# Routing totals from small matmuls, the key sums' column sums a step later, and one subtraction of the maxima per step

## The chip, the cores and the metric

The kernel runs on one core of a Trainium2 chip. The metric is the device time of one execution in microseconds. Five engines work side by side: TensorE (PE, with its weight loads listed apart as PEld), VectorE (DVE), ScalarE (ACT), GpSimd (POOL) and SyncE (SP), which issues most of the transfers. SBUF is the on-chip memory, PSUM the memory that TensorE writes its results to.

## The reference

Three layers follow one another. The first is linear attention with a softmax-like feature map, the second sends each token to one of eight experts, the third is a dense layer with a norm. Cut to what matters here:

```python
def phi(x):                                  # q, k: (8, 8, 576, 64), w_phi: (64, 128)
    proj = np.einsum('bhsd,df->bhsf', x, w_phi)
    proj = proj - np.max(np.abs(proj), axis=-1, keepdims=True)
    return np.concatenate([np.exp(proj), np.exp(-proj)], axis=-1)
q_p, k_p = phi(q), phi(k)
kv = np.einsum('bhsf,bhsd->bhfd', k_p, v)
z = np.sum(k_p, axis=2)                      # sum over the keys
num = np.einsum('bhsf,bhfd->bhsd', q_p, kv)
den = np.einsum('bhsf,bhf->bhs', q_p, z)[..., None] + 1e-06
x = num / den                                # 4608 tokens of 512

logits = x @ w_gate + modality_bias[modality_id]
e_idx = np.argmax(logits, axis=1)            # one expert of 8 for each token
gate_w = softmax(logits)[arange(N), e_idx]
for e in range(E):                           # w1[e]: 512 x 1024, w2[e]: 1024 x 512
    out[mask] = gate_w[mask, None] * (np.maximum(x[mask] @ w1[e], 0.0) @ w2[e])
# then h = out @ w_in, h * softmax(h), a norm, @ w_out
```

## The kernel before, in words

The attention part fills the first 347 us or so. Its work comes in 8 units (a pair of batch entries `p2` and one of two groups of four heads `g`); a unit has two halves (the two batch entries) and 9 jobs, and each job is one step of the main loop, so there are 72 steps. A step does the following. `project` multiplies a piece of keys and a piece of queries by `w_phi` (16 matmuls, L186) into the PSUM tile `pj`. DVE takes the largest absolute value of each group of 128 features (L191) and `features` subtracts it from `pj`, once for the keys (`xsk`) and once for the queries (`xsq`), both L196. ACT takes the two exponentials of the keys (`e`, L203 and L204). Two steps later (`LAGF`) `q_features` transposes the queries (L256) and ACT takes their exponentials (`qp`, L263), and `accum_kv` adds keys times values to the PSUM tile `kv` (L209). POOL adds the key features to a running sum `es` (L248; L224 for the 64 leftover rows of two batch entries), which starts as zeros (L217).

When a half is complete, `finish_kv` copies `kv` to `kt` on ACT (L251) and puts items on a list: two `kf_part` (kind "f", L330, copied to `kf` by ACT, L334), one `z_part` and four or five `tokens`, all of kind "64". `z_part` is 32 matmuls of one column each with `es` as weights (L310, "tp<-used,es" in the rows, called the z columns here); `es` must be complete for them. `tokens` multiplies 128 tokens' `qp` by `kf` (64 matmuls in two halves of PE, L310, "tp<-kf,qp"), and DVE divides by the denominator and writes the token rows `xt` and the gate logits `gs` (L409 to L415). At most two items of kind "64" (`COLS`) and two "f" (`FULL`) run in a step. `z_part` is ready one step after its half is complete.

After the second unit of a pair, `gating` runs for 4 or 5 token tiles (9 times in all; 36 tiles): DVE finds the expert of each token as a one-hot table `oh` (L427 to L441), two matmuls (L449 with a triangle of ones, L450 with all ones) count the tokens of the same expert ahead of each token in its tile, and in the whole tile; both go to one PSUM tile `rkp`, which ACT copies to `rk` (L455). DVE then runs a chain over the tiles: `base` starts as the running totals `cnt` (L468), each tile's totals are added to the one before (L470, one operation for a tile), and the sum of `rk` and `base` (L475) gives each token's place, with which POOL scatters the rows to the table `xe` in HBM (L482, `g_dsti` holds the places).

After the gating of the fifth batch pair's second half, `early.pick` (L694 to L706, tiles `ea_`) chooses the expert whose weights are loaded first; its result `ea_tab` is read by SP, which then issues the loads of these weights into `ldk`, `ldq` and `ldv` (L733, in `prefetch`, step `PRE` of the last unit). At step `STEP0` of the last unit the first weight tile is split into a rounded part on ACT (L776) and the rest on DVE (L777). `setup_bias` computes the routing bias on POOL at step `BIAS` (L103 to L113). The last tiles run in `finish_last`, with the first expert's matmuls (`first_slot`, L515, and its maximum with zero on DVE, L519) between them. From about 360 us on PE runs the expert and dense matmuls (L932), which the change does not touch.

PE's order is the order of the code in the attention part. DVE, ACT, POOL and SP get their order there from the compiler's scheduler, so an edit moves instructions on them that it does not name. PSUM tiles of the names `tp` come from a pool of 3 (`tps`), `pj` of 2, `kv` of 1.

## Time and profile before

| what | value |
|---|---|
| time, median of 3 runs | 1204.37 us (1201.35 to 1208.66) |
| profiled execution, own time | 1209.89 us |
| its span in the trace | 1207.7 us |
| mean granted clock of TensorE | 0.985 |
| PE busy | 1166.4 us (97%) |
| DVE busy | 842.5 us (70%) |
| ACT busy | 576.9 us (48%) |
| POOL busy | 404.1 us (33%) |

PE is busy nearly all the time, but the 41 us in which it is idle lie almost wholly in the first 360 us, so the views to read are those of that part: the timeline of PE with the idle time ahead of each operation and what ended it, and the windows, where PEclk tells at what share of full speed the clock was granted (about 0.5 is 1.2 GHz, 1.00 is 2.4 GHz). The profiled execution was 5.5 us slower than the median run.

### The profile page before, as it was taken

Reading aid. Unit: us, or ns where it says so; the run is one execution under the profiler, and the core shown is the slowest. Engines: PE = TensorE matmul, PEld = TensorE weight load, DVE = VectorE, ACT = ScalarE, POOL = GpSimd, SP = SyncE. Lnnn points to the kernel's source line nnn. Section 1 sums busy time; section 2 is a strip of 40 time slices with the busy share of each in tenths; the row PEclk is TensorE's granted clock in tenths of the full one; section 3 lists DMA queues with packets and bytes.
Section 4 is the critical chain, followed back from the end, with each engine's and each line's share of the span. In section 5 each row is a group of like instructions: output and inputs, shape, how many; then the busy total and the mean of one; then the engine's idle time right before and its main releaser. Section 6 shows DMA issues by size and latency. Waiting matters only on the chain.

```text
span 1207.7 us, 27753 instructions
## 1 busy us (share of the span) xinstructions
PE 1166.4 (97%) x10658; PEld 1017.8 (84%) x10658; DVE 842.5 (70%) x1606; ACT 576.9 (48%) x974; POOL 404.1 (33%) x460
## 2 busy tenths in 40 slices
PE   7998999997989999999999999999999999999997
PEld 5787887886879999999999999977777778888885
DVE  6689889798666577787777877665655565566561
ACT  6455554655443455555555654643434343444342
POOL 4967867866640000000000000123233333433331
PEclk9899999999899999999999999999999999999999
DMA  9523433332231322145231324787877856556541
GB/s 322 181 80 123 137 95 120 123 122 80 86 111 62 83 86 71 53 133 166 57 85 54 88 67 129 200 206 206 226 202 202 224 136 149 147 134 151 148 119 48
DMA packets 249657, 157.40 MB, mean 130 GB/s; under 512 B 168752, under 2 KB 227376, under 8 KB 249520
## 3 DMA queue, kind: packets, MB, share of 16 engines
q1 hardware_dynamic: 243472, 136.39, 41.4%
q0 software_dynamic: 5760, 19.03, 4.1%
q8 instruction: 86, 1.41, 0.5%
q14 instruction: 51, 0.42, 0.1%
q10 hardware_dynamic: 288, 0.16, 0.0%
HBM read 167.12 MB, written 51.37 MB: 181 GB/s over the span
## 4 chain that ended last, share of the span: by engine, by line
PE 41%; DMA 6%; issue 1%; ACT 1%; DVE 1%; SPq 1%; POOLq 0%; ACTq 0%; DVEq 0%
PE tp L932 20%; PE h L932 19%; DMA turned<-whi 2%; DMA wlo<-turned 2%; DMA gd<-xe 1%; PE tp L1251 1%; SPq L1102 1%; DMA ldk<-in_moe_w_dram 1%; PE tp L747 0%; DMA gt<-gd 0%; DMA yd<-yo 0%; PE tp L1235 0%; DMA out_dram<-wab,gt 0%; ACT ex L1121 0%; ACT whi L1153 0%
## 5 line engine op out<-in xcount | busy, mean ns | idle before, releaser
L777 POOL TENSOR_TENSOR yTl<-yin,yTh 128x512 fp32r<-128x512 f32 x36 | 47.4, 1317 | 415.4 <-PE tp L932 403.1
L248 POOL TENSOR_TENSOR es<-es,e 128x512 f32<-128x512 f32 x128 | 162.1, 1273 | 50.6 <-ACT e L204 43.4
L932 PE MATMUL tp<-xTh,whi 128*128 128x256 f32 x432 | 122.1, 283 | 2.3 <-PEq L1332 2.3
L932 PE MATMUL h<-hTh,wlo 128*128 128x256 f32 x432 | 120.4, 279 | 0.8 <-DVE wlo L777 0.8
L932 PE MATMUL h<-hTl,whi 128*128 128x256 f32 x432 | 120.5, 279 | 0.4 <-DVE hTl L947 0.4
L932 PE MATMUL tp<-xTl,whi 128*128 128x256 f32 x432 | 120.9, 280 | 0.0
L932 PE MATMUL tp<-xTh,wlo 128*128 128x256 f32 x432 | 120.9, 280 | 0.0
L932 PE MATMUL h<-hTh,whi 128*128 128x256 f32 x432 | 120.3, 279 | 0.0
L191 DVE TENSOR_REDUCE m<-pj 128x8 f32<-128x1024 f32 x72 | 87.7, 1219 | 40.7 <-PE pj L186 39.8
L263 ACT ACTIVATE qp<-tp 128x512 f32<-128x512 f32 x128 | 69.1, 593 | 71.8 <-PE tp L256 68.9
L1121 ACT ACTIVATE ex<-h,s_mx,gt 128x1024 f32<-128x1024 f32 x36 | 43.5, 1208 | 124.1 <-DVE s_mx L1118 66.8
L1116 DVE TENSOR_REDUCE s_mx<-h 128x1 f32<-128x512 f32 x72 | 46.4, 686 | 78.6 <-PE h L932 78.6
L1134 POOL TENSOR_SCALAR rs<-s_var,gt 128x1 f32<-128x1 f32 x36 | 12.4, 344 | 227.1 <-ACT sq L1131 227.1
L1131 ACT ACTIVATE sq<-ex 128x1024 bf16<-128x1024 f32 x36 | 38.1, 1058 | 97.9 <-DVE ex L1128 97.9
L932 PEld LDWEIGHTS tp<-xTh,whi 128*128 128x128 f32 x432 | 81.9, 189 | 2.5 <-issue 2.4
L932 PEld LDWEIGHTS h<-hTh,wlo 128*128 128x128 f32 x432 | 81.9, 190 | 0.9 <-DVE wlo L777 0.9
L932 PEld LDWEIGHTS tp<-xTh,wlo 128*128 128x128 f32 x432 | 82.5, 191 | 0.0
L932 PEld LDWEIGHTS tp<-xTl,whi 128*128 128x128 f32 x432 | 82.0, 190 | 0.0
L932 PEld LDWEIGHTS h<-hTl,whi 128*128 128x128 f32 x432 | 81.1, 188 | 0.7 <-DVE hTl L947 0.6
L932 PEld LDWEIGHTS h<-hTh,whi 128*128 128x128 f32 x432 | 81.2, 188 | 0.0
L310 PEld LDWEIGHTS tp<-kf,qp 128*64 128x64 f32 x2048 | 70.6, 136 | 8.4 <-issue 3.1
L310 PE MATMUL tp<-kf,qp 128*64 128x73 f32 x2048 | 72.7, 227 | 2.0 <-DVE g_base L468 0.9
(377 smaller groups left out, 3384.5 us busy)
## 6 DMA issues: line engine op xcount, KB each, us to landing
ldk<-in_moe_w_dram SPq DMA_DIRECT2D x66, 512.0 KB
ldv<-in_moe_w_dram SPq DMA_DIRECT2D x66, 512.0 KB
ldq<-in_moe_w_dram SPq DMA_DIRECT2D x44, 512.0 KB
turned<-whi SPq DMA_DIRECT2D x35, 512.0 KB
wlo<-turned SPq DMA_DIRECT2D x140, 128.0 KB
yin<-yd SPq DMA_DIRECT2D x18, 512.0 KB
yd<-yo SPq DMA_DIRECT2D x35, 256.0 KB
ldv<-in_v_dram SPq DMA_DIRECT2D x16, 512.0 KB
```

The costliest lines, as they stand in the source:

```text
L191: V.tensor_reduce(out=m, in_=pj, axis=AX.X, op=ALU.max, apply_absolute_value=True)
L248: G.tensor_tensor(out=eo, in0=eo, in1=ev[:, :, r, :], op=ALU.add)
L263: A.activation(u.qp[half][:, fh, 2 * hp : 2 * hp + 2, o : o + 2 * P], tp.rearrange("p (h r) t -> p h (r t)", r=2), AF.Exp, scale=sc,)
L310: T.matmul(out(rows, h, fh), lhsT=lhsT(side, rows, h, fh), rhs=rhs(side, h, fh), start=h == 0 and fh == 0, stop=fh == 1, skip_group_check= ...
L777: eng.tensor_tensor(out=lo, in0=src, in1=hi.bitcast(F32), op=ALU.subtract)
L932: T.matmul(o, lhsT=l, rhs=r, start=first and n == 0, stop=last and n == 2, skip_group_check=True)
L1102: SP.dma_start(out=lv[g], in_=dv[g])
L1116: V.tensor_reduce(out=mx, in_=h[:, sl], axis=AX.X, op=ALU.max, negate=True)
L1121: A.activation(ex, h, AF.Exp, bias=mx, scale=g, accum_out=sm)
L1131: A.activation(sq, ex, AF.Square, accum_out=var)
L1134: G.tensor_scalar(out=rs, in0=var, scalar1=g, scalar2=g, op0=ALU.mult, op1=ALU.mult)
L1251: T.matmul(b[group(g), dh, :], lhsT=ht[fh][:, f, group(g)], rhs=m.w1c(j % 2 * NMINI + g)[:, f, :], start=j == f == 0, stop=fh == 1 and f = ...
```

## The change

Line numbers fall by one to three behind the first edits; those of the changed kernel stand here in brackets where it helps. (1) `project` makes one subtraction for keys and queries together, 128 by 1024 (L193), into one tile `xs` of four buffers in place of `xsk` (3) and `xsq` (4) of half the size. `xt1` has 2 buffers in place of 3, and the last tile's `x0T` uses an `xs` buffer. (2) `z_part` is ready two steps after its half is complete and not one, except in the last unit and in the half that precedes `early.pick`. The tokens of the half wait for it, and so does the gating behind them. (3) `gating` sums the running totals on PE: the triangle matmul (L448) and then one matmul of all ones for each of the n tiles (L453), each added to all later tiles' columns, so that column block n of `rkp` holds the totals. DVE adds the old totals to it straight from PSUM (L458 for `cnt`, L460 for the places). The ACT copy, the chain L468 and L470 and L475 are gone; `counted` is called earlier in the code. (4) `STEP0` is 8 in place of 6.

```diff
--- before.py
+++ after.py
@@ -46,7 +46,7 @@
 FSTEP = 2
 RING = 5
 RING0 = 1
-STEP0 = 6
+STEP0 = 8
 POOL_FIRST = ()
 LOOK = 4
 MANUAL = {mybir.EngineType.PE, mybir.EngineType.Activation, mybir.EngineType.DVE, mybir.EngineType.Pool}
@@ -189,16 +189,15 @@
                     )
         m = w3p.tile([P, 2, 2, 2], F32, name="m")
         V.tensor_reduce(out=m, in_=pj, axis=AX.X, op=ALU.max, apply_absolute_value=True)
-        return [(nm, i, features(pj[:, :, a], m[:, :, a], nm)) for a, (nm, i) in enumerate(jobs)]
-
-    def features(pj, m, kind):
-        x = w3p.tile([P, 4, F], F32, name="xs" + kind, bufs=4 if kind == "q" else 3)
+        x = w3p.tile([P, 8, F], F32, name="xs", bufs=4)
         V.tensor_tensor(
-            out=x.rearrange("p (j r) f -> p r j f", r=2), in0=pj,
-            in1=m.unsqueeze(3).broadcast_to([P, 2, 2, F]), op=ALU.subtract,
+            out=x.rearrange("p (aj r) f -> p r aj f", r=2), in0=pj.rearrange("p r a j f -> p r (a j) f"),
+            in1=m.rearrange("p r a j -> p r (a j)").unsqueeze(3).broadcast_to([P, 2, 4, F]), op=ALU.subtract,
         )
-        if kind == "q":
-            return x
+        xs = [x[:, 4 * a : 4 * a + 4] for a in range(2)]
+        return [(nm, i, keys(x) if nm == "k" else x) for (nm, i), x in zip(jobs, xs)]
+
+    def keys(x):
         e = w3p.tile([P, 4, 2, F], F32, name="e", bufs=4)
         A.activation(e[:, :, 0, :], x, AF.Exp)
         A.activation(e[:, :, 1, :], x, AF.Exp, scale=-1.0)
@@ -337,7 +336,8 @@
         at = step[0]
         u.kf[half] = w2p.tile([P, 2, 4, HW], F32, name="kf")
         after = [Item("f", lambda j=j: kf_part(u, half, j)) for j in range(2)]
-        after.append(Item("64", lambda: z_part(u, half), ready=lambda: step[0] > at))
+        soon = u is last_unit() or u.p2 == 2 and u.g == half == 1
+        after.append(Item("64", lambda: z_part(u, half), ready=lambda: step[0] > at + (not soon)))
         if u is last_unit() and half:
             items.insert(0, items.pop())
             return
@@ -388,7 +388,7 @@
         if u.g == 0:
             if a == 0:
                 w = 1 if part == 2 else 4
-                t = xp.tile([P, w, ROW], F32, name=f"xt{w}")
+                t = xp.tile([P, w, ROW], F32, name=f"xt{w}", bufs=3 if w == 4 else 2)
                 t0 = 9 * u.p2 + i
                 G.tensor_copy(t[:, :, DM + 1 : DM + 2].bitcast(I32), c.tok[:, t0 : t0 + w].unsqueeze(2))
                 G.memset(t[:, :, DM + 2 : ROW], 0.0)
@@ -444,15 +444,22 @@
         )
         yield "0", 0
         yield "f", 2
-        rkp = tps.tile([P, 2, n, E], F32, name="tp")
-        ohf = oh.rearrange("p t e -> p (t e)")
-        T.matmul(rkp[:, 0].rearrange("p t e -> p (t e)"), lhsT=c.tri_bf, rhs=ohf, start=True, stop=True, skip_group_check=True)
-        T.matmul(rkp[:, 1].rearrange("p t e -> p (t e)"), lhsT=c.ones_bf, rhs=ohf, start=False, stop=True, skip_group_check=True)
-        rk = w("rk", [P, 2, 5, E])[:, :, :n, :]
-        if tiles[0] == 7:
-            V.tensor_copy(rk, rkp)
-        else:
-            A.copy(rk, rkp)
+        rkp = tps.tile([P, n + 1, E], F32, name="tp")
+        T.matmul(
+            rkp[:, 0:n].rearrange("p t e -> p (t e)"), lhsT=c.tri_bf, rhs=oh.rearrange("p t e -> p (t e)"),
+            start=True, stop=True, skip_group_check=True,
+        )
+        for a in range(n):
+            T.matmul(
+                rkp[:, a + 1 : n + 1], lhsT=c.ones_bf, rhs=oh[:, a : a + 1].broadcast_to([P, n - a, E]),
+                start=False, stop=True, skip_group_check=True,
+            )
+        old, cnt[0] = cnt[0], w("cnt", [P, E])
+        V.tensor_tensor(out=cnt[0], in0=rkp[:, n], in1=old, op=ALU.add)
+        rkb = w("rkb")[:, :n, :]
+        V.tensor_tensor(out=rkb, in0=rkp[:, 0:n], in1=old.unsqueeze(1).broadcast_to([P, n, E]), op=ALU.add)
+        if counted:
+            counted()
         sm = w("sm", [P, 5])[:, :n]
         V.tensor_reduce(out=sm, in_=ex, axis=AX.X, op=ALU.add)
         V.tensor_scalar(out=sm, in0=sm, scalar1=1e-9, scalar2=None, op0=ALU.add)
@@ -464,15 +471,6 @@
                     xs[part][:, i0 - lo : i1 - lo, DM : DM + 1], sm[:, i0 - tiles[0] : i1 - tiles[0]].unsqueeze(2)
                 )
         yield "0", 1
-        base = w("base", [P, 6, E])
-        V.tensor_copy(base[:, 0, :], cnt[0])
-        for a in range(n):
-            V.tensor_tensor(out=base[:, a + 1, :], in0=rk[:, 1, a, :], in1=base[:, a, :], op=ALU.add)
-        cnt[0] = base[:, n, :]
-        if counted:
-            counted()
-        rkb = w("rkb")[:, :n, :]
-        V.tensor_tensor(out=rkb, in0=rk[:, 0], in1=base[:, :n, :], op=ALU.add)
         V.tensor_tensor(out=rkb, in0=rkb, in1=oh, op=ALU.mult)
         dst = w("dst", [P, 5])[:, :n]
         V.tensor_reduce(out=dst, in_=rkb, axis=AX.X, op=ALU.add)
@@ -503,7 +501,7 @@
         tp = tps.tile([P, 4, P], F32, name="tp")
         for j in range(4):
             T.transpose(tp[:, j, :], m.x0[:, j * P : (j + 1) * P], c.ident)
-        m.x0T = w3p.tile([P, 4, P], F32, name="xsk")
+        m.x0T = w3p.tile([P, 8, P], F32, name="xs", bufs=4)[:, 0:4]
         A.copy(m.x0T, tp)
         m.xT(tps, 1)
         m.load_raw(7, m.e0)
```

The order on PE around a z column and the totals that follow two steps after `kf_part` (second pair of batch entries): before, then after. `es` is the sum of the key features, `used` the constants, `g_oh` the one-hot table.

```order
L209 MATMUL kv<-e,ldv 64x256 x4
L310 MATMUL tp<-used,es 64x1 x16
L186 MATMUL pj<-wphi,ldk 128x128 x4
L186 MATMUL pj<-wphi,ldq 128x128 x4
L256 MATMUL tp<-kept,xsq 128x128 x4
L449 LDWEIGHTS used
L449 MATMUL tp<-g_oh,used 128x40
L450 LDWEIGHTS used
L450 MATMUL tp<-g_oh,used 128x40
L209 MATMUL kv<-e,ldv 64x256 x4
L310 MATMUL tp<-kf,qp 64x73 x32
```

```order
L208 MATMUL kv<-e,ldv 64x256 x4
L186 MATMUL pj<-wphi,ldk 128x128 x4
L186 MATMUL pj<-wphi,ldq 128x128 x4
L255 MATMUL tp<-kept,xs 128x128 x4
L208 MATMUL kv<-e,ldv 64x256 x4
L309 MATMUL tp<-used,es 64x1 x16
L186 MATMUL pj<-wphi,ldk 128x128 x4
L186 MATMUL pj<-wphi,ldq 128x128 x4
L255 MATMUL tp<-kept,xs 128x128 x4
L448 LDWEIGHTS used
L448 MATMUL tp<-g_oh,used 128x40
L453 LDWEIGHTS used
```

The z columns (L310, now L309) stand behind one more projection, transpose and `kv`; the totals moved by a step as well, and four more matmuls L453 follow the last row.

The order on ACT around the first split of weights (`w_4661<-ldk`, now `w_4598`), in the last unit:

```order
L203 ACTIVATE e<-xsk 128x4x128
L204 ACTIVATE e<-xsk 128x4x128
L776 CAST w_4661<-ldk 128x1024
L263 ACTIVATE qp<-tp 128x2x256 x2
L251 COPY kt<-kv 128x512
L203 ACTIVATE e<-xsk 128x4x128
```

```order
L202 ACTIVATE e<-xs 128x4x128
L203 ACTIVATE e<-xs 128x4x128
L262 ACTIVATE qp<-tp 128x2x256 x2
L250 COPY kt<-kv 128x512
L774 CAST w_4598<-ldk 128x1024
L202 ACTIVATE e<-xs 128x4x128
```

The split stood ahead of two `qp` exponentials and of the copy to `kt`; now it stands behind both.

The order on DVE from the totals to the start of `early.pick` (`ea_num`), in the last unit's first steps:

```order
L470 TENSOR_TENSOR g_base<-g_rk,g_base 128x8 x2
L409 TENSOR_SCALAR r<-tp 128x4
L470 TENSOR_TENSOR g_base<-g_rk,g_base 128x8
L410 RECIPROCAL r<-r 128x4
L470 TENSOR_TENSOR g_base<-g_rk,g_base 128x8
L411 TENSOR_TENSOR gs<-tp,r 128x32
L415 TENSOR_TENSOR xt_4163<-tp,r 128x256
L470 TENSOR_TENSOR g_base<-g_rk,g_base 128x8
L475 TENSOR_TENSOR g_rkb<-g_rk,g_base 128x40
L694 TENSOR_TENSOR ea_num<-g_base,kept 128x8
```

```order
L191 TENSOR_REDUCE m<-pj 128x8
L458 TENSOR_TENSOR g_cnt<-tp,g_cnt 128x8
L460 TENSOR_TENSOR g_rkb<-tp,g_cnt 128x40
L193 TENSOR_TENSOR xs<-pj,m 128x2x4x128
L692 TENSOR_TENSOR ea_num<-g_cnt,kept 128x8
L474 TENSOR_TENSOR g_rkb<-g_rkb,g_oh 128x40
L693 TENSOR_REDUCE ea_mx<-ea_num 128x1
L476 TENSOR_REDUCE g_dst<-g_rkb 128x5
L694 SCALAR_TENSOR_TENSOR ea_num<-ea_num,ea_mx,kept 128x8
```

Five L470 with token work between them are replaced by L458 and L460, which stand behind one reduction of the projections more; the pick starts right behind the next subtraction.

## Rows read from the trace of the kernel before

**Rows 1.** Page, busy time of each engine over the span.

```profile
PE 1166.4 (97%) x10658; PEld 1017.8 (84%) x10658; DVE 842.5 (70%) x1606; ACT 576.9 (48%) x974; POOL 404.1 (33%) x460
```

**Rows 2.** Windows: length, busy of PE, PEld, DVE, ACT, POOL, PEclk, DMA, GB/s.

```profile
117.70:121.00 3.30, 3.30 (x22) 2.33 (x20) 3.17 (x6) 2.72 (x7) 2.62 (x3) 0.53 0.69 214
198.50:203.00 4.50, 4.50 (x44) 3.48 (x43) 3.32 (x5) 3.05 (x8) 4.09 (x4) 0.62 0.57 177
298.00:309.00 11.00, 10.21 (x80) 8.08 (x81) 6.48 (x9) 6.00 (x14) 5.97 (x5) 0.53 0.24 77
```

**Rows 3.** Timeline of PE, the z columns: start, length, operation, [idle before <-releaser].

```profile
32.81 1.88 PE L310 MATMUL tp<-used,es 128*64 128x1 f32 x32 [4.85 <-POOL es L224]
...
115.78 1.10 PE L310 MATMUL tp<-used,es 128*64 128x1 f32 x32 [2.31 <-POOL es L248]
...
173.56 1.10 PE L310 MATMUL tp<-used,es 128*64 128x1 f32 x32 [0.53 <-issue]
...
197.57 1.10 PE L310 MATMUL tp<-used,es 128*64 128x1 f32 x32 [1.59 <-issue]
...
278.47 1.10 PE L310 MATMUL tp<-used,es 128*64 128x1 f32 x32 [1.36 <-issue]
```

**Rows 4.** Timeline of PE, a step around 280 us; totals before kv, then two token tiles.

```profile
279.50 0.71 PE L186 MATMUL pj<-wphi,ldk 64*128 64x128 f32 x8
...
281.23 1.08 PE L209 MATMUL kv<-e,ldv 128*64 128x256 f32 x8
282.14 2.20 PE L310 MATMUL tp<-kf,qp 128*64 128x73 f32 x64
```

**Rows 5.** Timeline of PEld, the weight loads of the two totals matmuls.

```profile
280.98 0.10 PEld L449 LDWEIGHTS <-used 128*128 128x128 bf16 x1
281.09 0.10 PEld L450 LDWEIGHTS <-used 128*128 128x128 bf16 x1
```

**Rows 6.** Page, section 5: the token matmuls and the reduction of the projections.

```profile
L310 PE MATMUL tp<-kf,qp 128*64 128x73 f32 x2048 | 72.7, 227 | 2.0 <-DVE g_base L468 0.9
...
L191 DVE TENSOR_REDUCE m<-pj 128x8 f32<-128x1024 f32 x72 | 87.7, 1219 | 40.7 <-PE pj L186 39.8
```

**Rows 7.** Timeline of PE, the wait for kt.

```profile
298.79 2.29 PE L330 MATMUL tp<-used,kt 128*128 128x144 f32 x8 [4.46 <-ACT kt L251]
```

**Rows 8.** Timeline of ACT, the first weight split and what follows.

```profile
296.23 1.04 ACT L776 CAST w<-ldk 128x1024 fp32r<-128x1024 f32 x1 [4.00 <-DMA ldk<-in_moe_w_dram]
...
298.15 0.59 ACT L251 COPY kt<-kv 128x512 f32<-128x512 f32 x1
```

**Rows 9.** Timeline of DVE, from the totals to the split.

```profile
283.18 2.12 DVE L470 TENSOR_TENSOR g_base<-g_rk,g_base 128x8 f32<-128x8 f32 x2
...
290.16 0.16 DVE L706 CAST ea_tab<-ea_res 128x2 int32<-128x2 f32 x1
...
297.31 1.23 DVE L777 TENSOR_TENSOR w<-ldk,w 128x1024 fp32r<-128x1024 f32 x1 [2.93 <-ACT w L776]
```

**Rows 10.** Timeline of POOL, head, middle and tail of the attention part.

```profile
30.43 4.75 POOL L224 TENSOR_TENSOR es<-es,e 64x1024 f32<-64x1024 f32 x2
35.26 0.68 POOL L109 TENSOR_TENSOR bias<-msk,mb 128x288 f32<-128x288 f32 x1
...
282.75 3.89 POOL L248 TENSOR_TENSOR es<-es,e 128x512 f32<-128x512 f32 x3
...
324.88 1.00 POOL L482 DMA_INDIRECT xe<-xt,g_dsti  x1 [3.08 <-DMA gd<-xe]
...
328.44 8.63 POOL L248 TENSOR_TENSOR es<-es,e 128x512 f32<-128x512 f32 x7
```

**Rows 11.** Groups by line on DVE, the first 360 us: busy, mean ns.

```profile
L196 DVE TENSOR_TENSOR xsk<-pj,m 128x512 f32<-128x512 f32 x72 | 49.6, 691 | 5.0 <-ACT qp L263 0.5
...
L470 DVE TENSOR_TENSOR g_base<-g_rk,g_base 128x8 f32<-128x8 f32 x36 | 20.4, 565 | 0.5
L411 DVE TENSOR_TENSOR gs<-tp,r 128x32 f32<-128x32 f32 x72 | 13.7, 190 | 2.2
```

## The prediction

> **What bounds the kernel now.** PE is busy 1166.4 us [rows 1] of a span of 1207.7, so 41 us are idle, and a change to work on DVE, ACT or POOL pays only where PE waits for it, or where PE gets less or more to do. I therefore read the timeline of PE first, with the idle time ahead of each operation, and looked there for the operations that the change moves. Six of the z columns that it defers have a wait ahead of them [rows 3]: the first of all waits 4.85 us for POOL's add of the leftover keys, one waits 2.31 us for POOL's sums and one 1.59 us; one of 0.53 us is the last of three alike (0.51 and 0.40 us at 91.05 and 134.72 us), 1.44 us together. The row at 278.47 us, 1.36 us, is the sixth of them in order of use. The other deferred z columns have no wait. The largest wait outside them is 4.46 us for `kt` at 298.79 us [rows 7]. Then I read the windows, since a wait can cost twice: behind the 2.31 us wait the clock was 0.53 over 3.3 us, behind the 1.59 us wait 0.62 over 4.5 us, and behind the wait for `kt` 0.53 over 11 us [rows 2]. Between its two levels, 1.2 and 2.4 GHz, that lost 3.3 x 0.47 = 1.55, 4.5 x 0.38 = 1.7 and 11 x 0.47 = 5.2 us. No window of lowered clock stands behind the waits of 0.4 to 0.53 us and of 1.36 us. Last I read what PE's waits hang on: POOL's adds, ACT's split of the first weights and the chain on DVE ahead of it [rows 8 to 10].
>
> **The change part by part.** *The z columns a step later.* A step of projection, transposes and `kv` takes 282.14 - 279.50 = 2.6 us on PE [rows 4]. POOL gets these 2.6 us more, and each steady wait (2.31, 1.59, 0.53, 0.51, 0.40 us) is shorter, so I take all five as gone: 5.3 us. With the two larger ones I take their slow windows as gone: 1.55 + 1.7 = 3.3 us. Bounds: nothing of the 3.3 if something else keeps the clock down. The tokens of the half move a step too; at most two of them run in a step, as before, so PE has the same work in another order.
>
> The first z columns wait for POOL's L224, which started at 30.43 us; behind it stood the two bias products (L109, 0.68 us each) [rows 10]. In the new order of POOL these two stand ahead of L224, so `es` is ready 1.3 us later, while PE comes 2.6 us later: a gain of 2.6 - 1.3, about 1.2 us. Bounds: 0, if the bias table lands later than the masks did, and 2.6.
>
> *The totals.* A gating of n tiles has n + 1 matmuls in place of 2; over 36 tiles and 9 gatings that is 36 + 9 - 18 = 27 more. The two loads of weights start 0.11 us apart [rows 5], so they cost 27 x 0.11 = 3.0 us of PE. Nothing hides them. What they remove is off PE: the L470 chain was 36 operations of 565 ns, 20.4 us of DVE [rows 11], with pairs at 2.12 us while POOL's adds ran (283.18 us in [rows 9], 282.75 us in [rows 10]). The 18 adds that replace chain and L475 read PSUM; the nearest row with a PSUM source is 190 ns (L411, [rows 11]), 3.4 us for 18 if nothing holds them. PE had waited 0.9 us in front of token tiles for DVE at that chain [rows 6]; I count 0.9 as gone.
>
> *The subtraction.* Two of 691 ns (the second alike) become one of 1024 elements, which I price like the reduction of 1024 elements, 1219 ns ([rows 6, 11]): 0.16 us x 72 = 12 us of DVE. The reduction's idle time is 39.8 us of waiting for PE, so DVE is the one that waits and this brings PE nothing by itself. The key exponentials start some 0.5 us later (1219 against 691 ns); the matmuls on them come two steps later, and that hides it.
>
> *The weights' split.* Before, PE reached L330 at 298.79 - 4.46 = 294.3 us, but `kt` stood behind the split on ACT, and the split stood idle for `ldk` until 296.23 us [rows 7, 8]. The new order has `kt` first, so that wait can't be for `kt`. But the last token tile's DVE reads stand behind the split's second half (L777) on DVE, and its PSUM tile is the one that the second `kf_part` needs (three tiles in turn). So the same load is still waited for, one matmul group later. When does it land? `ea_tab` was written at 290.16 us and the split started at 296.23, 6.1 us later [rows 8, 9]. The totals ended at 281.23 us; without the 1.36 us wait, one step later and with four more matmuls they end at 281.23 - 1.36 + 2.6 + 0.4 = 282.9. The pick took 290.16 - 281.23 = 8.9 us from there, and 2.1 us of it and more were stretched L470. The shortest that I see is the end of the two token tiles behind which its last cast now stands, 282.9 + 0.9 + 2.1 = 285.9 us [rows 4], and with the tiles' own reads 287.0. The pick's operations now run where POOL's adds run, and two stretched ones add 2.1: 289.0. PE reaches L330 at 294.3 - 1.36 + 0.4 = 293.4. Then `ldk` lands at 293.1 to 295.1; 1.04 us on ACT, 1.23 us on DVE and some 0.8 us of token reads put the second `kf_part` at 296.2 to 298.2 and its end 0.6 us behind. Before, it would have ended at 298.79 + 1.1 at full speed. That is 1.1 to 3.1 us earlier, the 1.36 us included; I take 2.0, and leave the slow window of 5.2 us in place. Bounds: -2, if the pick takes 8.9 us again (291.8, and 301.6 at the end), and the whole wait gone (below).
>
> Which of the pick's operations POOL's adds hold can't be seen before, since it ran behind them; L470, with both inputs in SBUF, took 1.06 us a piece beside them [rows 9, 10], and L411, with one in PSUM, 190 ns [rows 11]. The Trainium skill ("SBUF — State Buffer", section "Who interferes with whom") says that a DVE instruction with two SBUF inputs contends with POOL's reads, and one with a single SBUF input does not. By it the pick's two first combinations of two SBUF tiles are held and little else, which gives the 289.0; were all held until POOL's 3.89 us of adds are over, it would be some 2 us later and the sum 1199.
>
> *The tail.* POOL's last adds are 8.63 us from 328.44 us, and the last unit's z columns, which are not deferred, end with them. Three scatters stand ahead now, from 324.88 us, and four after the change, each 1.00 us and 0.3 us until the next [rows 10]: 1.3 us later. The second maximum with zero of `first_slot` also moves behind six small operations on DVE, of some 0.1 us each: 0.6 us. Together -2.0 us, between 0 and -4 (if the clock falls there, by 1.7 us as above).
>
> **The sum**, against the profiled execution: 5.3 + 3.3 + 1.2 + 0.9 + 2.0 - 3.0 - 2.0 = 7.7 us, from 1209.9 to 1202.2. That execution was 5.5 us above the median run; on the median of 1204.4 the sum gives 1196.7, **1197 us**.
>
> **The rivals.**
> - *The wait for the first weights goes whole.* If `ea_tab` is early enough (by about 284.8 us: the second `kf_part` is reached at 293.4 + 0.6, less 6.1, 1.04, 1.23 and 0.8), PE meets no wait at L330 and the clock stays up: 4.46 + 1.36 + 5.2 = 11.0 us in place of the 2.0 counted, 9 more: **1188**. For it: the chain loses its stretched adds. Against it: the totals themselves come a step later, and the pick reads behind two token tiles.
> - *The early part's gain is eaten at the split and by the clock.* The pick runs beside POOL's adds and takes 8.9 us as before (-2 in place of 2.0), and a lowered clock stays in both early windows (0 in place of 3.3): 7.7 - 4.0 - 3.3 = 0.4 us, **1204**. For it: every operation of the pick reads SBUF, and POOL adds for 3.89 us there [rows 10].
> - *The totals' PSUM tile blocks PE.* The tile was freed by an ACT copy; now DVE frees it, in its own queue. Three PSUM tiles go round: totals, two token tiles, then the next transposes take the totals' one again. That leaves `kv` 0.9, tokens 2.1 and a projection 1.1, about 4 us, for DVE to come. Before, DVE began on the totals 283.18 - 281.23 = 2.0 us after them [rows 4, 9]; from a lag of 4 us on PE waits. If the lag became 6 us, seven steady gatings would wait 2 us each, 14 us more than the sum: **1211**, slower than before. The new order has one more reduction ahead of the add, 1.2 us, which brings the lag to 3.2 us, short of the point.
> - *The deferral does nothing*, because POOL falls back by a step as well. POOL works 404 of 1208 us and waits for ACT's features between its adds, so it isn't behind for good; the sum would lose 8.6 us and be 1205. I count it with the second.
>
> **How the numbers follow.** My forecast, with 1193 to 1201 for its own spread, 0.50; the wait gone whole 0.15; the gain eaten 0.25; the blocked tile 0.10. What a measurement of this kernel can tell from no change is about 0.5%, 6 us, so faster means below 1198.4. Of the forecast's 0.50 I put 0.35 there, since its centre lies 1.7 us inside: faster 0.35 + 0.15 = 0.50, same 0.15 + 0.25 = 0.40, slower 0.10. The range goes from the second case's 1188, a little lower for its own spread, 1187, up to 1206, which takes in the eaten gain and the deferral that does nothing, and leaves out the blocked tile and what of the first rival lies lower.
>
> **What would show it.** In the profile of the changed kernel: z columns without idle time except the first, which keeps about 3.6 us; PEclk 0.9 and more in the slices around 118 and 200 us; L448 and the L453 behind it 0.11 us apart; L458 and L460 near 0.2 us, beside POOL's adds as well; at L330 in the last unit a wait of 3 to 5 us that ends with DVE (`xt`) and no longer with `kt`; the last z columns with 1 to 2 us of wait for POOL. The prediction is wrong if a wait of over 1 us remains on the deferred columns, if PE waits for L458 or L460, or if `ea_tab` comes before 285 or after 290 us on a trace that is else shifted by under 10 us.

## The result and the profile after

The changed kernel took 1191.11 us (median of 4 runs, 1190.17 to 1192.98) against 1204.05 us before: 12.9 us less, a ratio of 0.989 (95% interval 0.987 to 0.991). That is inside the stated range, and on the far side of the forecast of 1197 us. In a later set of runs, on another chip, the same kernel took 1211.58 us beside 1211.41 us before (ratio 1.000, 0.997 to 1.003); what stood between the two is told below.

The page of the changed kernel, busy times over its span of 1188.4 us, against [rows 1]:

```profile
PE 1159.4 (98%) x10685; PEld 1013.3 (85%) x10685; DVE 827.9 (70%) x1497; ACT 576.6 (49%) x966; POOL 400.8 (34%) x460
```

PE is 7 us less busy though it has 27 matmuls more: less of its time is at the lower clock (the mean granted clock is 0.991, before 0.985). DVE is 14.6 us less busy.

The steady z columns (all but the first and the last unit's) have no idle time ahead of them any more (against [rows 3]). The first ones keep a wait, and so do the last ones, in the timeline of PE of the changed kernel:

```profile
32.37 1.10 PE L309 MATMUL tp<-used,es 128*64 128x1 f32 x32 [1.03 <-POOL es L223]
...
322.01 1.10 PE L309 MATMUL tp<-used,es 128*64 128x1 f32 x32 [0.27 <-POOL es L247]
```

Windows of 20 us, the changed kernel (two rows) and then the one before (length, busy of PE, PEld, DVE, ACT, POOL, PEclk, DMA, GB/s):

```profile
20.00:40.00 20.00, 18.96 (x241) 14.22 (x241) 13.03 (x16) 12.29 (x26) 15.47 (x15) 0.91 1.03 338
280.00:300.00 20.00, 16.81 (x205) 13.42 (x204) 12.19 (x22) 9.43 (x18) 8.63 (x8) 0.77 0.37 119
```

```profile
20.00:40.00 20.00, 15.15 (x166) 11.39 (x164) 9.09 (x12) 9.65 (x20) 15.00 (x15) 0.83 1.03 341
```

The granted clock over 20 to 40 us rose from 0.83 to 0.91, which is 1.6 us of PE by itself. From 280 to 300 us it is still at 0.77: the wait for the first weights is not gone, only moved. The timeline of PE there, with the totals and the two waits:

```profile
268.65 0.18 PE L448 MATMUL tp<-g_oh,used 128*128 128x40 bf16 x1 [0.48 <-ACT qp L262]
268.67 0.27 PE L453 MATMUL tp<-g_oh,used 128*128 128x40 bf16 x5
268.87 1.08 PE L208 MATMUL kv<-e,ldv 128*64 128x256 f32 x8
...
278.69 1.85 PE L309 MATMUL tp<-kf,qp 128*64 128x73 f32 x32 [2.61 <-DVE xt L415]
...
282.99 0.66 PE L329 MATMUL tp<-used,kt 128*128 128x144 f32 x4
286.83 1.30 PE L329 MATMUL tp<-used,kt 128*128 128x144 f32 x4 [3.19 <-DVE xt L415]
```

The six matmuls of the totals take 268.87 - 268.65 = 0.22 us. The two of before took 281.23 - 281.09 = 0.14 us and started 0.03 us apart, as the timeline of PE of before shows; the 0.11 us of [rows 5] lie between their weight loads:

```profile
281.09 0.18 PE L449 MATMUL tp<-g_oh,used 128*128 128x40 bf16 x1
281.12 0.18 PE L450 MATMUL tp<-g_oh,used 128*128 128x40 bf16 x1
```

In the changed kernel a token tile then waits 2.61 us for DVE, and the second `kf_part` 3.19 us, against 4.46 us for `kt` before [rows 7]. What DVE did in that time, and POOL beside it:

```profile
269.80 0.15 DVE L458 TENSOR_TENSOR g_cnt<-tp,g_cnt 128x8 f32<-128x8 f32 x1
269.87 0.19 DVE L460 TENSOR_TENSOR g_rkb<-tp,g_cnt 128x40 f32<-128x40 f32 x1
...
271.52 1.23 DVE L694 SCALAR_TENSOR_TENSOR ea_num<-ea_num,ea_mx,kept 128x8 f32<-128x8 f32 x1
...
273.00 1.10 DVE L696 TENSOR_SCALAR ea_num<-kept,ea_mx 128x8 f32<-128x8 f32 x1
...
274.57 2.01 DVE L698 SCALAR_TENSOR_TENSOR ea_base<-ea_num,kept 128x8 f32<-128x8 f32 x1
...
276.74 1.17 DVE L704 CAST ea_tab<-ea_res 128x2 int32<-128x2 f32 x1
```

```profile
265.40 5.21 POOL L247 TENSOR_TENSOR es<-es,e 128x512 f32<-128x512 f32 x4
...
271.45 2.62 POOL L247 TENSOR_TENSOR es<-es,e 128x512 f32<-128x512 f32 x2
...
275.27 2.62 POOL L247 TENSOR_TENSOR es<-es,e 128x512 f32<-128x512 f32 x2
```

The two adds from PSUM (L458, L460) took 0.15 and 0.19 us in the middle of POOL's adds from 265.40 to 270.6 us. Four operations of the pick (L694, L696, L698 and L704, `ea_` tiles) took 1.10 to 2.01 us beside POOL's adds from 271.45 and 275.27 us. So `ea_tab` was written by 277.9 us, 9.0 us behind the totals, as before (290.16 + 0.16 - 281.23 = 9.1 us [rows 4, 9]), and ACT's split waited for the load until 283.54 us (against 296.23 in [rows 8]):

```profile
283.54 1.04 ACT L774 CAST w<-ldk 128x1024 fp32r<-128x1024 f32 x1 [7.84 <-DMA ldk<-in_moe_w_dram]
```

Positions tell where the time went. The table has the start of the query transposes of three steps and of the first expert matmul in the profiled executions, and the difference to the kernel before, all in us. At each of them PE has done the same matmuls in both kernels, but for those of the totals:

| place | before | changed | difference |
|---|---|---|---|
| behind the first z columns and their slow clock (step 14) | 70.18 | 65.99 | -4.19 |
| ahead of the deferred z columns that precede the first weights (step 59) | 273.45 | 258.80 | -14.65 |
| behind the wait for the first weights and the tokens behind it (step 68) | 333.21 | 319.16 | -14.05 |
| first expert matmul | 360.41 | 345.47 | -14.94 |

Right behind the wait (step 65) the difference is larger, 312.15 - 295.92 = 16.23 us, but the changed kernel has one token tile less behind it there: 64 matmuls, 2.2 us [rows 4], which it runs by step 68. The expert part itself is not touched; the profiled execution of before was 4.4 us longer there.

### The profile page after: what moved, and what is told of

Its sections match the earlier page's. It is cut to its first block, busy times and chain, and to the rows that moved or that the text cites. A ratio compares the mean times of both kernels' runs of the same rounds, so it can differ in the third digit from the quotient of the medians.

```text
span 1188.4 us, 27693 instructions
## 1 busy us (share of the span) xinstructions
PE 1159.4 (98%) x10685; PEld 1013.3 (85%) x10685; DVE 827.9 (70%) x1497; ACT 576.6 (49%) x966; POOL 400.8 (34%) x460
## 4 chain that ended last, share of the span: by engine, by line
PE 45%; DMA 3%; issue 1%; DVE 1%; ACT 1%; SPq 0%; POOLq 0%; ACTq 0%; DVEq 0%
PE tp L930 22%; PE h L930 21%; DMA turned<-whi 2%; DMA wlo<-turned 1%; PE tp L1249 1%; PE tp L745 0%; SPq L1100 0%; PE tp L1233 0%; DMA out_dram<-wab,gt 0%; ACT ex L1119 0%; DVE ex L1124 0%; DVE whi L1094 0%; DVE ex L1126 0%; DVE s_mx L1114 0%; ACT wab L1161 0%
## 5 line engine op out<-in xcount | busy, mean ns | idle before, releaser
L193 DVE TENSOR_TENSOR xs<-pj,m 128x1024 f32<-128x1024 f32 x72 | 88.1, 1224 | 4.9
L309 PEld LDWEIGHTS tp<-kf,qp 128*64 128x64 f32 x2048 | 70.3, 137 | 11.0 <-issue 5.0
```

The costliest lines, as they stand in the source:

```text
L193: V.tensor_tensor(out=x.rearrange("p (aj r) f -> p r aj f", r=2), in0=pj.rearrange("p r a j f -> p r (a j) f"), in1=m.rearrange("p r a j - ...
L309: T.matmul(out(rows, h, fh), lhsT=lhsT(side, rows, h, fh), rhs=rhs(side, h, fh), start=h == 0 and fh == 0, stop=fh == 1, skip_group_check= ...
```

## The experiments

The first four ran in one set, beside the kernel before at 1205.71 us (19 runs), the next four in a second set on the same chip 24 minutes later, beside 1214.24 us (13 runs), the last four on another chip beside 1211.41 us (7 runs). Ratios are to the kernel before of the same set. The changed kernel itself ran in the third set and, ahead of the first, beside 1204.05 us; in the first two sets it is compared by the ratios. Positions are of one profiled execution each.

**The z columns not deferred.**

```diff
-ready=lambda: step[0] > at + (not soon)
+ready=lambda: step[0] > at
```

> The changed kernel with the z columns one step after their half again, all else as changed. Theory (the deferral pays): the first z wait of 4 to 5 us, the waits of 2.3 and 1.6 us and the slow clock behind the three come back, 9 to 12 us, so 1200 to 1203 us. Rival (the time that totals and subtraction free on DVE pays, and the deferral only moves work): DVE still has 14 us less to do, so most of the gain stays, 1192 to 1195 us.

Measured: 1193.75 us (4 runs, two at 1190 and two at 1197 to 1198; the profile is one of the longer two), ratio 0.990 (0.985 to 0.995). The theory that the deferral pays falls: without it nearly all of the gain is still there. But at step 59 this kernel was only 1.8 us ahead of the one before, where the changed one was 14.7 ahead; by the first expert matmul it was 8.5 us ahead. It gains 6.0 us at the first weights (steps 59 to 65). Its timeline of PE has the old z waits, shorter (the last deferred one 0.36 in place of 1.36 us), and 2.54 us for `kt`:

```profile
275.66 1.10 PE L309 MATMUL tp<-used,es 128*64 128x1 f32 x32 [0.36 <-POOL xt L470]
...
278.30 0.27 PE L453 MATMUL tp<-g_oh,used 128*128 128x40 bf16 x5
...
293.24 2.29 PE L329 MATMUL tp<-used,kt 128*128 128x144 f32 x8 [2.54 <-ACT kt L250]
```

Its pick ran a step earlier, where POOL added less, and none of its own operations took over 0.23 us; one cast of the gating between them (L478) took 1.14 us beside an add. In the timeline of DVE L694 takes 0.22 and L704 0.17 us:

```profile
280.76 0.22 DVE L694 SCALAR_TENSOR_TENSOR ea_num<-ea_num,ea_mx,kept 128x8 f32<-128x8 f32 x1
...
281.01 1.14 DVE L478 CAST g_dsti<-g_dst 128x5 int32<-128x5 f32 x1
...
283.26 0.17 DVE L704 CAST ea_tab<-ea_res 128x2 int32<-128x2 f32 x1
```

From the totals (278.5) to `ea_tab` (283.4) it took 4.9 us, not 9.0.

**The deferral alone, in the kernel before.**

```diff
-after.append(Item("64", lambda: z_part(u, half), ready=lambda: step[0] > at))
+soon = u is last_unit() or u.p2 == 2 and u.g == half == 1
+after.append(Item("64", lambda: z_part(u, half), ready=lambda: step[0] > at + (not soon)))
```

> The kernel before with the deferral of the z columns alone. Theory (the deferral pays): 9 to 12 us faster than before, 1192 to 1195 us, with no wait ahead of the steady z columns and at most some 2 us ahead of the first. Rival (DVE's freed time pays): 0 to 3 us faster, 1201 to 1204 us, with the waits moved to the token tiles behind DVE's totals chain.

Measured: 1202.18 us (10 runs), ratio 0.997 (0.995 to 0.999): 3.5 us, the rival's number, and its mechanism. The steady z columns have no wait, but the token tiles behind them now wait for DVE's chain of totals, twice 2.8 us, here the first, and one tile 3.40 us for the pick. By the positions the whole gain is at the first z columns (66.32 against 70.18 us at step 14); from there to step 59 it took 203.8 us, before 203.3:

```profile
100.51 2.47 PE L310 MATMUL tp<-kf,qp 128*64 128x73 f32 x64 [2.81 <-DVE g_base L469]
```

**The totals as before, in the changed kernel.** The two matmuls, `A.copy(rk, rkp)` and the chain L468 to L475 take the place of L448 to L460; the rest stays.

> The changed kernel with the totals as before: two matmuls a gating, ACT's copy to SBUF, the chain of adds on DVE. Theory: the added matmuls cost little (some 0.05 us a piece in the new trace, 1.4 us in all), and the chain gives back the 0.3 us waits of three gatings with what hangs on them, 1.5 us, and a later pick: 1 to 4 us slower than the changed kernel, 1192 to 1195 us. Rival (the matmuls are 0.11 us each as forecast, and the chain is covered): 1 to 2 us faster than the changed kernel, 1189 to 1190 us.

Measured: 1201.45 us (10 runs), ratio 0.997 (0.995 to 0.999), 4.3 us less than before, where the changed kernel took 12.9 us less beside its own runs of before; so the totals are worth some 9 us once the z columns are deferred, far more than expected. From step 14 to step 59 it took 200.0 us, the changed kernel 192.8. PE's waits at the token tiles, in two places alike:

```profile
97.73 1.24 PE L309 MATMUL tp<-kf,qp 128*64 128x73 f32 x32 [0.62 <-DVE xt L415]
...
100.78 1.24 PE L309 MATMUL tp<-kf,qp 128*64 128x73 f32 x32 [1.81 <-DVE xt L415]
```

**Two subtractions a step, in the changed kernel.**

```diff
-V.tensor_tensor(out=x[...8 groups...], in0=pj, in1=m, op=ALU.subtract)
+for a, (nm, _) in enumerate(jobs):
+    V.tensor_tensor(out=x[...4 groups...], in0=pj[:, :, a], in1=m[:, :, a], op=ALU.subtract)
```

> The changed kernel with two subtractions a step, 128 by 512 each. Theory: DVE is the one that waits for PE in most of the steps, so 12 us of DVE more cost nothing or up to 2 us where DVE is 95 to 98% busy (around 100 to 120, 180 to 200, 260 to 280 us): 1191 to 1193 us. Rival (DVE's time pays): 4 to 8 us slower, 1195 to 1199 us.

Measured: 1188.66 us (4 runs), ratio 0.987 (0.983 to 0.990). The rival falls; the two subtractions, 0.69 and 0.68 us in place of one of 1.22, 11 us in all, cost nothing. By the ratios it is even some 3 us better than the changed kernel. Part of that can be read: the scheduler set POOL's bias products behind the add of the leftover keys again, and the first z columns did not wait at all; behind them (step 8) this kernel was 2.75 us ahead of the changed one. At the first weights (steps 59 to 65) it gained 3.5 us more, with less time at the slow clock; in the expert part it took 3.6 us longer. Its timeline of POOL:

```profile
27.76 0.21 POOL L103 CAST modf<-mod 128x36 f32<-128x36 int32 x1 [4.50 <-DMA mod<-in_moe_modality_id_dram]
...
28.64 4.77 POOL L225 TENSOR_TENSOR es<-es,e 64x1024 f32<-64x1024 f32 x2
33.49 0.68 POOL L109 TENSOR_TENSOR bias<-msk,mb 128x288 f32<-128x288 f32 x1
```

**The old chain, read from PSUM.** In the kernel with the old totals:

```diff
-rk = w("rk", [P, 2, 5, E])[:, :, :n, :]
-if tiles[0] == 7:
-    V.tensor_copy(rk, rkp)
-else:
-    A.copy(rk, rkp)
+rk = rkp
```

> The changed kernel with the old two matmuls and the old chain of one add a tile, but with the adds reading the totals straight from PSUM (ACT's copy to SBUF left out), so that each add has one input in SBUF and one in PSUM. Theory (POOL's adds hold a DVE add with two inputs in SBUF, and this cost the old chain its time): the chain's adds take 0.15 to 0.2 us each beside POOL's adds, PE's waits for DVE at the token tiles (1.8 us twice, 1.2 and 3.7 us with the old totals) go, and the time is near the changed kernel's, 1191 to 1195 us. Rival (the number of steps in the chain costs, whatever the adds read): near the old totals, 1198 to 1202 us.

Measured: 1207.28 us (10 runs), ratio 0.995 (0.994 to 0.997). By the ratio it stands near the old totals, on the rival's side. But the set was slower as a whole, and the profile has 7.2 us of idle time inside PE's matmuls that nothing recorded ends (told below), where those of the first set have next to none; so this alone decides nothing, and it was run again beside the other two kernels.

**The split held back.** In `split`, with `after` an element of the last unit's first `kf`:

```diff
+if after is not None:
+    self.tc.nc.scalar.copy(hi[:, 0:1], after)
 self.tc.nc.scalar.copy(hi, src)
```

> The changed kernel with the first weight split held back behind the last unit's first kf copy, by one element written to its tile from there. Theory (PE's 3.2 us wait in the last unit is for the DVE reads behind the split): the wait goes and with it the slow clock after it (0.77 over 20 us, 4.6 us): 1184 to 1188 us. Rival (the wait turns into another one, for the later loads, the split or the first rows at the end of the attention part): 1190 to 1192 us.

Measured: 1203.13 us (4 runs), ratio 0.991 (0.989 to 0.994); the next kernel, from the same set, is the measure, since the changed kernel itself did not run in it. At step 59 it was 2.1 us behind that kernel, behind the first weights (step 65) 4.3 us ahead: 6.4 us gained, within the 3 to 7 us expected, with no wait at `kf_part`. At the first expert matmul it was 1.15 us ahead: the rest is the rival's share. The two medians are the same (1203.13 and 1202.86 us). The last z columns now come before POOL's adds, and behind their short waits the clock falls. Its timeline of PE and its windows:

```profile
331.49 1.02 PE L309 MATMUL tp<-used,es 128*64 128x1 f32 x16 [0.77 <-POOL es L247]
332.36 4.14 PE L309 MATMUL tp<-kf,qp 128*64 128x73 f32 x64
```

```profile
330.00:335.00 5.00, 4.15 (x76) 4.09 (x78) 0.34 (x2) 0.75 (x3) 1.35 (x2) 0.64 0.09 31
335.00:340.00 5.00, 5.00 (x96) 4.92 (x93) 3.40 (x19) 0.23 (x1) 0.00 (x0) 0.67 0.00 0
```

10 us at 0.64 and 0.67 lose 3.4 us.

**The loads of the routing bias first.**

```diff
+bias = late()
 zero = w1p.tile([P, ROW], F32, name="zero")
```

> The changed kernel with the two loads of the routing bias issued ahead of the eight writes of zeros. Theory (POOL stands 4 us idle for the modality numbers, and the first sum of the keys stands behind them): no wait ahead of the first z columns (1.0 us) and little of the slow clock there (0.91 over 20 us, 1.8 us): 1188 to 1190 us. Rival (the clock is low there for another cause, or the loads that are pushed back cost as much): 1191 us.

Measured: 1202.86 us (4 runs), ratio 0.991 (0.988 to 0.994). The first z columns did not wait, and at step 14 this kernel was 5.05 us ahead of the one above (3.79 us of wait there, and its slow clock). So the theory holds for the cause; what it is worth against the changed kernel depends on how long that one's wait is, which with the same instruction order was 1.03 us in one profile and 3.02 us in another.

**Without four of POOL's adds beside the pick.** The adds of the first two key pieces of the last unit, two for each, are left out, so that part of the key sums is missing and the routing of its tokens with it; the expert part takes another time for that reason, and only the trace up to 300 us is used.

```diff
-for r in range(2):
+for r in range(0 if u is last_unit() and i < 2 else 2):
```

> The changed kernel without POOL's adds of the first two key pieces of the last unit, which run beside the pick of the first expert (this part of the last unit's key sums is left out). Theory (these adds hold the pick's operations, four of them for 1.1 to 2.0 us): no operation of the pick over 0.3 us, the table of the pick some 4 us earlier, the 2.6 us wait at the token tile gone and the 3.2 us wait at the weights' split down to under 1.5 us, with a shorter slow clock: 1183 to 1188 us. Rival (the pick is late because the totals come a step later): 1190 to 1192 us.

Measured: the run's time (1284.73 us) has another routing in it. Two operations early in the pick (L692, L694) were still held, beside adds of POOL that stayed in (2.63 us from 284.21 us). Two later ones, which were long in the changed kernel, are 0.16 and 0.17 us:

```profile
284.68 0.83 DVE L692 TENSOR_TENSOR ea_num<-g_cnt,kept 128x8 f32<-128x8 f32 x1
...
285.76 1.09 DVE L694 SCALAR_TENSOR_TENSOR ea_num<-ea_num,ea_mx,kept 128x8 f32<-128x8 f32 x1
...
287.73 0.16 DVE L697 TENSOR_SCALAR ea_rest<-ea_num 128x8 f32<-128x8 f32 x1
...
288.12 0.17 DVE L704 CAST ea_tab<-ea_res 128x2 int32<-128x2 f32 x1
```

In the changed kernel (third set, with the first two at 0.83 and 1.09 us as here) they were 1.91 and 1.10 us:

```profile
293.59 1.91 DVE L697 TENSOR_SCALAR ea_rest<-ea_num 128x8 f32<-128x8 f32 x1
...
295.73 1.10 DVE L704 CAST ea_tab<-ea_res 128x2 int32<-128x2 f32 x1
```

So it is POOL's adds that hold them. The time from the totals to `ea_tab` fell from 8.2 us there to 5.5 us, not by the 4 us expected, and the wait at the token tile went, as expected. The wait at `kf_part` did not: it grew to 4.96 us, since PE came there earlier and the load still takes 6.5 us from `ea_tab`, the split and the reads another 3.3.

```profile
298.05 1.30 PE L329 MATMUL tp<-used,kt 128*128 128x144 f32 x4 [4.96 <-DVE xt L415]
```

From the totals to the second `kf_part` it took 298.05 - 282.61 = 15.4 us, 18.0 in the changed kernel of the third set. The faster pick alone did not remove this wait.

**Three of them again, on one chip, and a combination.**

> The changed kernel itself, beside the three next ones on one chip, since the kernel before took 1205 us in the company of the first experiments and 1214 us in that of the second. Either theory: 0.987 to 0.992 of the kernel before on this chip, some 13 us less.

Measured: 1211.58 us (4 runs), ratio 1.000 (0.997 to 1.003). Outside what either theory said: the gain was gone. The timeline of PE shows where, in the token tiles behind each gating:

```profile
99.89 0.37 PE L309 MATMUL tp<-kf,qp 128*64 128x73 f32 x5 [0.38 <-issue]
100.65 0.36 PE L309 MATMUL tp<-kf,qp 128*64 128x73 f32 x4 [0.39 <-issue]
102.08 0.87 PE L309 MATMUL tp<-kf,qp 128*64 128x73 f32 x20 [1.06 <-issue]
```

The matmuls of one tile come in small groups, some 0.7 us and more from the start of one to the start of the next, with gaps that nothing recorded ends; all 64 of each tile are in the trace. Between 40 and 345 us they add up to (line, releaser, total, times, longest), with 0.6 us ahead of two z columns among them:

```profile
PE tp L309 <- issue: 10.6, 21, 1.1
```

Four windows of 20 us at a clock of 0.91 behind them (100 to 140 and 180 to 220 us) lose another 7.2 us. The two medians of this one kernel lie 20.5 us apart. In its two profiles 20.0 us lie between step 14 and step 59 (192.8 and 212.8 us), and 10.0 + 7.2 = 17.2 us of these are the gaps and the clock; the rest is not accounted for. All profiles of the second and third set have such gaps (4.6 to 10.6 us with those in other matmuls, 1.1 to 10.0 us in the token tiles alone); the first profile of the changed kernel and those of the first set have none in the token tiles. It isn't the chip alone, since the first two sets ran on one.

> The changed kernel with the totals as before (ACT's copy, the chain of adds from SBUF), beside the changed one on one chip. Theory (the deferred tokens meet DVE late, since POOL's adds hold the chain): 8 to 12 us slower than the changed kernel of this chip. Rival (the 10 us seen before were the chip's): within 3 us of it.

Measured: 1216.56 us (4 runs), 5.0 us slower than the changed kernel beside it, between the theory and the rival; about half of what the first set showed, with fewer of the gaps (5.1 us against 10.6).

> The old chain of one add a tile, reading the totals from PSUM, beside the two others on one chip. Theory (what costs is that POOL's adds hold a DVE add with two inputs in SBUF): within 4 us of the changed kernel, and 5 us or more faster than the old totals. Rival (the number of adds in the chain costs): within 3 us of the old totals.

Measured: 1208.66 us (4 runs), 7.9 us faster than the old totals and 2.9 faster than the changed kernel. The theory holds: with one add a tile and two matmuls, but from PSUM, the chain costs nothing, and that with more of the gaps than the old totals had (9.1 us against 5.1). The edit also takes ACT's copy off the path, and what that is worth by itself was not run; the adds themselves show the hold, with 11 of 36 over 0.3 us from SBUF, 17.2 us in all, and none over 0.17 us from PSUM, 5.8 us in all. The adds in the kernel with the old totals, and here (line, times min/median/max in ns):

```profile
L470 DVE TENSOR_TENSOR g_base<-g_rk,g_base x36: 149/168/2327, 92.3 to 362.9; 128x8 f32<-128x8 f32 x36
```

```profile
L466 DVE TENSOR_TENSOR g_base<-tp,g_base x36: 155/166/168, 94.9 to 361.1; 128x8 f32<-128x8 f32 x36
```

> The changed kernel with two subtractions a step, the loads of the routing bias ahead of the writes of zeros, and the first weight split held back behind the last unit's first kf copy. Theory (the first wait and the wait for the first weights are the two large ones left, 1 to 4 us and 3 to 4 us with their slow clocks, and some 3 us come back at the last z columns): 4 to 9 us faster than the changed kernel of this chip. Rival (the waits move to the end of the attention part in full): within 2 us of the changed kernel with two subtractions, that is 2 to 3 us faster than the changed one.

Measured: 1190.08 us (4 runs, 1187.84 to 1193.46), ratio 0.982 (0.979 to 0.985): 21.5 us faster than the changed kernel beside it and 21.3 faster than before, the best of all here. It has no wait at the first z columns and none at `kf_part`; a token tile still waits for DVE behind the pick:

```profile
283.08 1.24 PE L311 MATMUL tp<-kf,qp 128*64 128x73 f32 x32 [2.41 <-DVE xt L417]
```

It also had fewer of the gaps (4.6 us of them between 40 and 345 us, against 10.6), and how much of the 21.5 us is due to the edits and how much to the gaps was not separated.

The edit of `STEP0` was not run by itself: with 6 in place of 8 the order of instructions on all five engines is the same, so it has no part in the difference.

## Why the prediction came out as it did

The sign, the range and most of the places were right; the attribution was not. The sum has 7.7 us, the profiled executions show 14.9 us up to the first expert matmul.

- **The deferral of the steady z columns.** All six steady waits went (the 1.36 us one too, which the prediction counts with the first weights), and both slow windows with them, as forecast. But the step that counted 5.3 + 3.3 us for the deferral by itself failed: alone it brought 3.5 us, all of it at the first z columns, since the steady waits went to the token tiles, where DVE was late with its chain of totals (2.8 us twice). From step 14 to step 59 the profiled executions took 203.3 us before, 203.8 with the deferral alone, 200.2 with the new totals and no deferral, 200.0 with the deferral and the old totals, and 192.8 with both: of the 10.5 us there neither edit brings more than 3.3 without the other. What the deferral adds up to step 59 is mostly given back at the pick: without it the kernel gained 6.0 us at the first weights, and with it lost 0.6. The prediction asked what PE waits for today and not what it meets next; the rival that the deferral does nothing named POOL as the engine that falls back, and it was DVE.
- **The totals.** Counted as a loss of 3.0 against a gain of 0.9, they were the main part: undone, they cost some 9 us in the first set (12.9 against 4.3 us of gain) and 5 in the third, and with them but without the deferral the gain was still 12.0 us (1193.75 against 1205.71 us). Two terms were mis-sized. The added matmuls took 0.08 us for four (0.22 - 0.14), so about 0.5 us for 27, not 3.0: I priced them by the distance of two weight loads, 0.11 us, though the two matmuls themselves started 0.03 us apart. And the chain was valued at the waits that it caused while PE still waited elsewhere. What made it slow was not the number of its steps but where their operands lay, as the chain from PSUM showed.
- **The first z columns.** Forecast 1.2, measured 4.2 us at step 14. I had left out the slow clock behind the wait (1.6 us), and the modality numbers landed earlier in this execution than before (POOL's L103 at 27.82 against 29.55 us). In seven other profiles with the same order on POOL the wait was 1.94 to 3.79 us and not 1.03, and step 14 came 1.5 to 5.3 us earlier than before.
- **The subtraction.** Forecast nothing, and so it was: two cost nothing beside the new totals, and one brought 0.7 us beside the old ones (1202.18 against 1201.45 us), not clear of the noise. Its side effect on POOL's order at the head was seen in the order and priced at 1.3 us, and the kernel with two subtractions was 2.75 us ahead there.
- **The first weights.** The place was right: `kt` was no longer waited for, and the second `kf_part` was, for the reads behind the split; the slow clock there stayed, as forecast. The size was not: forecast 2.0 us earlier, measured 0.6 us later (-14.05 against -14.65), with the new 2.61 us wait at the token tile. The pick took 9.0 us, the second rival's figure, and not 4.1 to 6.1; by the prediction's own sign, `ea_tab` from 285 to 290 us in a trace that is not shifted, it came too late, at 277.9 + 14.7 = 292.6. The rule of the Trainium skill ("SBUF — State Buffer", section "Who interferes with whom") held for the adds from PSUM, 0.15 us beside POOL's adds, and for the combination of two SBUF tiles (L694, 1.23 us). But I had read it too narrowly: a copy with a cast (L704, 1.17 us) and an operation with a scalar (L696, 1.10 us) were held too. For a single SBUF input the same section excepts modes that use both of DVE's ports, and it names copy, cast and tensor_scalar as forms that can enter them when their operands meet its conditions; whether these did, no run here shows.
- **The tail.** Forecast a loss of 2.0, measured a gain of 0.9 (-14.94 against -14.05). The fourth scatter did put POOL's last adds 1.3 us later, as priced (timeline of POOL of the changed kernel, against [rows 10]: the scatters start 16.5 us earlier, the adds 15.2):

```profile
308.38 0.99 POOL L480 DMA_INDIRECT xe<-xt,g_dsti  x1 [2.31 <-DMA gd<-xe]
...
313.20 8.62 POOL L247 TENSOR_TENSOR es<-es,e 128x512 f32<-128x512 f32 x7
```

But the last z columns waited 0.27 us for them and not 1 to 2; before it was 0.27 and 0.43 us (timeline of PE of before):

```profile
336.06 0.63 PE L310 MATMUL tp<-used,es 128*64 128x1 f32 x16 [0.27 <-POOL es L248]
337.12 0.63 PE L310 MATMUL tp<-used,es 128*64 128x1 f32 x16 [0.43 <-POOL es L248]
```

Added up to the first expert matmul: 4.19 + 10.46 - 0.60 + 0.89 = 14.94 us, where the sum had 1.2 + 7.6 + 2.0 - 1.1 - 2.0 = 7.7 (the matmuls of each stretch at 0.11 us taken off). That the last two stretches together came out near their forecast is luck: +2.0 and -2.0 were both wrong in sign. The totals' PSUM tile never blocked PE: no wait on L458 or L460 in the profiles of the changed kernel.

That the same kernel later showed no gain was no case in the prediction. The gaps in the token tiles, with the slow clock behind them, took it back there; why they come in some sets and not in others is open. The kernel before was 7 to 10 us slower in those sets too, but there is no profile of it from them.

## What to carry to other kernels

When a wait is taken from the engine that sets the time, price what that engine meets next, in the same step, before the gain is counted: the deferral alone brought the steady part nothing (203.8 against 203.3 us), since the wait went to an engine that another edit had yet to free. When the positions of two kernels are compared, take places where the engine has done the same work in both: here one token tile would make a loss of 0.6 us look like a gain of 1.6. On VectorE beside a busy GpSimd, look at where an operation's inputs lie before its size: of the adds from SBUF some took 1 to 2.3 us, and with one input in PSUM none took over 0.17 us. And time a small gain in more than one set of runs, since gaps whose cause nobody has found can take it back.

## What the runs showed that was not expected

- Gaps inside a run of identical matmuls, 0.3 to 1.1 us, that nothing recorded ends, 10.0 us in one profile and none in another of the same kernel; with them the clock falls to 0.91 over 20 us.
- Small matmuls that go to the same PSUM tile from the same weights cost about 0.02 us more apiece (four for 0.08 us).
- VectorE operations of 2 to 40 elements a partition beside POOL's adds took up to 2.3 us (L470) where they take 0.15 to 0.2 us alone, and not only those with two SBUF inputs.
